# Eleven groups of unread matmuls added to TensorE's queue of a gated recurrence and convolution kernel

## Chip, cores and metric

The kernel runs on one core of one Trainium2 chip. The metric is the device time of one execution in microseconds (us), lower being better.

## What is computed

The input has 4 batches of 6336 steps by 256 channels. A gated linear recurrence runs along the steps, and its output goes through a gated unit with a causal convolution of five taps. Cut to what matters, the reference is:

```
log_a = 8 * sigmoid(r_gate) * log(a_base)            # a_base = sigmoid(a_param), per channel
a_t   = exp(log_a)
norm  = sqrt(max(1 - a_t*a_t, 1e-6))
h     = a_t[:, t] * h + (norm * sigmoid(i_gate) * x)[:, t]     # for each step t; y[:, t] = h
gate  = sigmoid(causal_conv(y, conv_w))              # five taps, per channel
out   = (gate * (y @ w_val)) @ w_out
```

## The kernel before

The 25344 rows (batch and step together) are cut into 51 windows `w` of 512 rows (256 for the first two and the last), and these into 28 chunks `c` of one or two windows. Inputs arrive with rows on the partitions. The recurrence needs channels on the partitions, so gates and products are turned by transposes on TensorE. The 256 channels are two halves `h`.

All work is issued in one order that is written out by hand: the string `ORDER` holds words such as `nt.3@6,7`, which is operation `nt` for chunk 3 in PSUM banks 6 and 7. Each word calls a function `op_...`. Every engine takes its own instructions in that order and waits at the first whose inputs are not ready; the DMA queue on SyncE (SP) does so too, with its loads and stores. The steps, with the engine and the line of the profile:

- `lr`, `li`, `lx` (SP, L290): load r_gate, i_gate and x of a window into rings of four windows. `st` (SP, L514) stores a window of the output.
- `ta`, `tb` (ScalarE, L308 and L311): tanh of half of r_gate and i_gate, for a chunk. `pp` and `up` (GpSimd, L318 and L330): 1 + tanh, and its product with x, into `uring`.
- `xp` and `uv` (TensorE L335, VectorE L344): the same product for the windows 1, 2 and 6, with x copied to PSUM by a float32 matmul with an identity.
- `tr` (TensorE, L355) transposes the tanh of r; `ex` (ScalarE, L371) makes a_t from it; `sq` (GpSimd, L379) squares it; `rt` (ScalarE, L398) makes the norm for a batch of chunks, with a table load before and after (L530).
- `nt` (TensorE, L413) transposes the norm back, `xg` (VectorE, L420) multiplies it into the products, `xt` (TensorE, L429) transposes those, and `sc` (VectorE, L451) runs the recurrence as a scan into `yring`.
- `cv` (TensorE, L463) is the convolution by matmuls with diagonal weights, `tg` (ScalarE, L470) its tanh, `vl` (TensorE, L478) is y @ w_val, `gv` (VectorE, L483) the gating, `ou` (TensorE, L493) the product with w_out; `cd` and `ca` (VectorE L501, ScalarE L503) copy the result from PSUM to be stored.

The eight PSUM banks are given to operations by the numbers behind the `@`. An operation that writes a bank waits until the earlier contents have been read.

Of the kernel before, what the change touches and what calls it, by code (L numbers as in the profile page):

```python
# [9 lines left out]
P = 128  # L10
# [30 lines left out]
s_wl.1 up.0 lx.1 ex.3.1 sq.3.0 lx.4 lx.3 tb.3 sq.3.1 ta.6 pp.4 sq.4.1 lr.13 ta.5 li.5 li.6 sq.4.0 li.7 xp.2@2,3  # L41
lr.14 pp.3 rt.0 tr.5.0@4,5 lx.6 uv.2 rt.2 up.4 nt.0@0 rt.1 xg.0 rt.3 xt.0@0,1 xp.1@2 sc.0.0 up.3 nt.1@3 lx.5 nt.2@0
uv.1 s_wl.0 xg.1 xg.2 xt.1@2,3 lx.7 sc.0.1 lr.12 nt.3@6,7 sc.1.0 lr.11 xt.2@0,1 sc.1.1 ex.5.0 xg.3 tr.5.1@2,3 li.8
sc.2.0 xt.3@6,7 ex.5.1 sq.5.0 cv.0@4,5 sc.2.1 tg.0 sc.3.1 cv.1@0,1 cv.2@4,5 tg.1 tb.4 s_wcast xp.6@0,1 sc.3.0 tg.2
li.10 li.9 pp.5 ta.8 vl.1@2,3 lx.10 vl.2@4,5 uv.6 sq.6.1 vl.0@6,7 ta.7 gv.2 lr.17 cv.3@0,1 lx.8 sq.6.0 gv.0
ou.2.0@4,5 gv.1 tb.5 ou.0.0@6 cd.2.0 ou.1.0@7 up.5 tr.7.0@2,3 tg.3 cd.0.0 st.2 vl.3@4,5 lr.16 cd.1.0 ex.7.0 sq.5.1
st.1 tr.7.1@0,1 gv.3 lr.15 st.0 nt.4@6,7 li.12 ex.7.1 pp.7 cv.4@2,3 xg.4 sq.7.0 ou.3.0@4,5 tg.4 vl.4@0,1 cd.3.0 tb.6
pp.8 xt.4@2,3 gv.4 st.3 sq.7.1 li.11 lr.18 sc.4.1 ou.4.0@0,1 li.13 lx.9 up.8 rt.4 sc.4.0 pp.9 up.7 cd.4.0 cv.6@2,3
st.4 vl.6@0,1 lx.12 pp.10 li.14 nt.5@4,5 lx.11 sq.8.0 cv.5@6,7 tg.6 xg.5 tb.7 up.10 gv.6 xt.5@4,5 ou.6.0@0,1 sc.5.0
ta.9 li.16 up.9 vl.5@2,3 tg.5 lr.19 cd.6.0 ta.10 pp.11 nt.6@6,7 gv.5 st.6 pp.12 li.15 xg.6 tb.8 ou.5.0@2,3 lr.22  # L50
up.11 tr.9.0@0,1 sc.5.1 ca.5.0 xt.6@6,7 ex.9.0 st.5 tr.9.1@2,3 lr.20 sc.6.0 lr.21 cv.7@4,5 ex.9.1 sq.8.1 up.12
cv.8@0,1 sc.6.1 tg.8 vl.7@2,3 pp.14 lx.16 lx.15 tg.7 nt.7@0,1 lx.14 sq.9.1 lx.13 tb.9 gv.7 cv.9@4,5 sq.10.1 xg.7
ou.7.0@2,3 tg.9 vl.9@6,7 cd.7.0 ta.11 sq.9.0 xt.7@4,5 gv.9 st.7 cv.10@2,3 li.20 ta.12 li.18 sc.7.0 pp.16 li.17
vl.8@6,7 sq.10.0 vl.10@0,1 tg.10 lr.26 li.19 gv.8 ou.9.0@2,3 pp.13 gv.10 ou.8.0@6,7 rt.5 up.14 cd.9.0 ou.10.0@0,1
tr.11.1@4 sc.7.1 st.9 up.16 lr.25 cd.10.0 cv.11@2,3 up.13 cd.8.0 st.10 nt.8@0,1 lr.23 tr.11.0@5 st.8 pp.15 xg.8
tg.11 vl.11@6,7 lr.24 lx.18 ex.11.1 up.15 xt.8@0,1 gv.11 lx.17 ex.11.0 nt.9@2,3 sc.8.0 sq.11.1 tb.10 cv.12@6,7
tr.12.0@5 xg.9 ex.12.0 li.22 pp.17 li.21 sc.8.1 tg.12 pp.18 ou.11.0@2,3 tb.11 xt.9@4,5 sq.11.0 vl.12@6,7 cd.11.0
cv.13@0,1 ta.14 sq.12.0 gv.12 st.11 li.23 cv.14@2,3 tg.13 sc.9.1 lr.29 pp.20 ou.12.0@6,7 ta.13 up.18 vl.13@0,1
cd.12.0 tr.12.1@5 tg.14 up.17 sc.9.0 st.12 tr.13.1@6,7 ex.12.1 lx.19 lx.20 nt.10@2,3 ex.13.1 li.24 sq.12.1 gv.13
tr.13.0@4,5 tb.12 xg.10 ou.13.0@0,1 sq.13.1 xt.10@2,3 cd.13.0 ex.13.0 cv.15@6,7 pp.22 sc.10.0 st.13 lx.21 cv.16@0,1  # L60
pp.19 lx.22 tg.15 lr.28 lr.30 sq.13.0 vl.15@4,5 tg.16 sc.10.1 li.25 vl.14@6,7 lr.27 pp.21 vl.16@0,1 gv.15 rt.6
sq.14.1 gv.14 ou.15.0@4,5 up.19 gv.16 cv.17@2,3 ou.14.0@6,7 cd.15.0 up.20 ou.16.0@0,1 cd.14.0 st.15 li.26 nt.11@4,5
cd.16.0 sq.14.0 lx.24 vl.17@6,7 tg.17 xg.11 st.14 lx.23 tb.13 st.16 gv.17 xt.11@4,5 up.21 cv.18@2,3 sc.11.1 sc.11.0
li.27 nt.12@6,7 li.28 ta.15 up.22 vl.18@0,1 tg.18 lr.32 pp.23 lr.31 ta.16 ou.17.0@2,3 pp.24 gv.18 up.24 tb.14 xg.12
tr.15.1@4,5 cv.20@0,1 cd.17.0 ex.15.1 xt.12@6,7 up.23 st.17 lr.33 tr.15.0@2,3 sc.12.0 lx.26 tg.20 lr.34 vl.20@4,5
sq.16.1 ex.15.0 cv.19@0,1 sc.12.1 sq.15.1 tg.19 ou.18.0@2,3 tb.15 cd.18.0 cv.21@6,7 pp.26 gv.20 st.18 sq.16.0
vl.19@2,3 tg.21 lx.25 lx.27 nt.13@0,1 ta.17 gv.19 lx.28 li.30 sq.15.0 vl.21@6,7 xg.13 li.29 ou.20.0@2,3 gv.21
xt.13@0,1 pp.27 rt.7 cv.22@4,5 cd.20.0 up.26 ou.21.0@6,7 sc.13.0 ou.19.0@2,3 pp.25 cd.19.0 up.25 sc.13.1 st.19 li.32
nt.14@2,3 up.27 lx.29 li.31 ta.18 lr.36 lx.30 cd.21.0 vl.22@0,1 lr.35 xg.14 pp.28 tg.22 tr.17.1@6,7 up.28 lr.38
tb.16 nt.15@2,3 gv.22 xt.14@4,5 lr.37 ex.17.1 tr.17.0@0,1 pp.29 xg.15 st.21 pp.30 sc.14.1 cv.23@2,3 ex.17.0 lx.31  # L70
up.29 cv.24@6,7 st.20 sc.14.0 tg.23 vl.23@0,1 sq.18.1 tb.17 li.34 ou.22.0@2,3 gv.23 up.30 li.33 nt.16@4,5 tg.24
cd.22.0 vl.24@0,1 lx.32 ta.19 ou.23.0@6,7 pp.31 xg.16 li.35 xt.15@2,3 sq.18.0 ca.23.0 gv.24 cv.26@4,5 li.36 ta.20
sc.15.0 sq.17.0 cv.25@0,1 st.22 tg.26 tr.19.0@6,7 sc.15.1 pp.32 lx.34 tg.25 vl.25@4,5 up.31 ex.19.0 tr.19.1@0,1
st.23 gv.25 ou.24.0@2,3 lr.41 ex.19.1 sq.19.0 xt.16@6,7 cd.24.0 ou.25.0@4,5 sc.16.0 st.24 cv.28@2,3 tb.18 lx.33
up.32 cv.27@0,1 tg.28 cd.25.0 tg.27 sq.19.1 vl.28@2,3 sc.16.1 st.25 lr.42 tb.19 vl.27@4,5 vl.26@0,1 sq.17.1 lr.39
gv.28 lr.40 gv.26 pp.34 ou.28.0@2,3 rt.8 lx.36 pp.36 gv.27 ou.26.0@0,1 pp.33 ou.27.0@4,5 up.34 cv.29@6,7 cd.28.0
cd.26.0 vl.30@2,3 up.33 cd.27.0 nt.17@0,1 tg.29 st.27 nt.18@4,5 pp.35 xg.17 lx.35 ta.22 st.28 vl.29@6,7 sq.20.1
xg.18 li.40 li.39 xt.17@0,1 li.38 gv.29 tr.22.0@4 sq.20.0 li.37 ta.21 sc.17.0 cv.30@6,7 st.26 up.36 tg.30 tr.21.1@5
sc.17.1 tr.21.0@0 lx.38 ex.22.0 xt.18@6,7 ex.21.0 tr.22.1@4 sq.22.0 lx.37 gv.30 ex.21.1 cv.31@0,1 lx.40 up.35
sc.18.0 ex.22.1 nt.19@2,3 lr.44 tg.31 cv.32@4,5 sq.22.1 sc.18.1 tb.21 ou.29.0@0,1 sq.21.1 tg.32 xg.19 ou.30.0@6,7  # L80
tb.20 vl.32@4,5 cd.29.0 sq.21.0 xt.19@2,3 gv.32 li.42 vl.31@0,1 lr.43 pp.38 li.41 cd.30.0 lx.39 lr.45 rt.9 up.38
gv.31 lr.46 sc.19.1 ou.31.0@0,1 st.29 pp.37 cv.33@6,7 pp.40 ou.32.0@4,5 cd.31.0 up.37 cd.32.0 cv.34@0,1 sc.19.0
nt.20@4,5 up.40 tg.33 lx.41 st.30 tg.34 li.43 vl.33@6,7 li.44 tb.22 xg.20 vl.34@0,1 pp.39 cv.36@2,3 nt.21@4,5 gv.33
up.39 ta.23 gv.34 ou.33.0@6,7 pp.41 ta.24 xg.21 lr.48 xt.20@0,1 lr.47 pp.42 st.31 cd.33.0 cv.35@4,5 lx.42 tg.36
sc.20.1 st.32 up.41 tr.23.0@6,7 tg.35 vl.35@2,3 ex.23.0 li.45 tr.23.1@4,5 gv.35 li.46 ex.23.1 sc.20.0 xt.21@6,7
sq.23.0 st.33 vl.36@2,3 tb.23 ou.34.0@4,5 sq.24.1 lx.43 gv.36 ou.35.0@0,1 sc.21.0 ca.34.0 cv.37@2,3 pp.44 ta.25
st.34 sq.23.1 cv.38@4,5 lx.44 sc.21.1 tg.37 tr.25.1@6 up.42 ex.25.1 nt.22@2,3 cd.35.0 tg.38 ou.36.0@6,7 sq.24.0
xg.22 sa.25.1 st.35 tr.25.0@0 lr.50 vl.38@4,5 lx.46 ex.25.0 cd.36.0 pp.43 xt.22@2,3 tb.24 gv.38 st.36 sq.25.0
cv.39@6,7 lx.45 sc.22.0 vl.39@4,5 tg.39 li.47 pp.46 vl.37@0,1 lr.49 up.43 ou.38.0@6,7 gv.37 rt.10 li.48 cd.38.0
ou.37.0@0,1 pp.45 sc.22.1 vl.40@6,7 up.44 gv.39 cv.40@2,3 up.46 cd.37.0 nt.23@4,5 st.37 cv.41@0,1 xg.23 tg.40 up.45  # L90
lx.48 st.38 lx.47 ta.27 tg.41 nt.24@2,3 gv.40 vl.41@4,5 xg.24 ta.26 tr.27.0@0 xt.23@6,7 gv.41 ex.27.0 ou.39.0@2,3
tb.25 sc.23.0 cv.42@4,5 ca.39.0 ou.41.0@0,1 pp.48 tg.42 sc.23.1 st.39 xt.24@2,3 pp.47 li.49 ca.41.0 li.50 tr.26.0@6
ou.40.0@4,5 up.48 ex.26.0 st.41 tr.26.1@0 sc.24.0 tr.27.1@1 ca.40.0 cv.44@6,7 ex.27.1 up.47 st.40 cv.43@4,5 ex.26.1
lx.49 sc.24.1 tg.44 sa.27.1 nt.25@0,1 sq.26.1 tg.43 vl.42@6,7 sq.27.0 tb.26 xg.25 vl.44@4,5 sq.26.0 tb.27 vl.43@2,3
gv.42 pp.50 xt.25@0,1 pp.49 gv.44 ou.42.0@6,7 rt.11 gv.43 ou.44.0@4,5 up.49 ca.42.0 sc.25.1 ou.43.0@2,3 ca.44.0
st.42 cv.45@6,7 ca.43.0 st.44 cv.46@4,5 sc.25.0 st.43 lx.50 nt.26@1 tg.46 vl.46@2,3 xg.26 tg.45 cv.47@4,5 gv.46
vl.47@6,7 tg.47 ou.46.0@2,3 gv.47 up.50 vl.45@4,5 ca.46.0 nt.27@6 ou.47.0@0,1 gv.45 st.46 xt.26@2,3 ca.47.0 xg.27
ou.45.0@4,5 sc.26.0 st.47 cv.48@0,1 ca.45.0 sc.26.1 xt.27@6,7 st.45 tg.48 vl.48@4,5 sc.27.1 cv.49@2,3 gv.48
vl.49@0,1 tg.49 sc.27.0 ou.48.0@4,5 gv.49 cv.50@2,3 ca.48.0 ou.49.0@0,1 tg.50 st.48 vl.50@4,5 ca.49.0 gv.50 st.49
ou.50.0@4 ca.50.0 st.50  # L100
"""


@with_exitstack
def kernel(
    ctx: ExitStack,
    tc: tile.TileContext,
    x: bass.AP,
# [8 lines left out]
    nc = tc.nc  # L117
# [36 lines left out]
    at = 4  # L154
    for c in range(NCH):
# [5 lines left out]
        if wrap:  # L161
            at = 4
# [7 lines left out]
        at = col  # L170
# [17 lines left out]
    with tc.manual_schedule():  # L188
# [11 lines left out]
        ident_b = const.tile([P, P], BF16, name="ident_b")  # L200
# [361 lines left out]
```

## Time and profile before

| quantity | value |
|---|---|
| median of 3 runs | 294.9 us (294.23 to 295.23) |
| profiled execution, its own time | 294.79 us |
| its span from the first to the last instruction | 292.8 us |
| mean granted TensorE clock | 0.983 |
| ScalarE busy | 274.1 us (94%) |
| VectorE busy | 246.9 us (84%) |
| GpSimd busy | 241.8 us (83%) |
| TensorE busy, matmuls | 241.5 us (83%), 2473 of them |
| DMA | 104.75 MB, 358 GB/s on average |

Busy times are of one profiled execution. The granted clock is TensorE's share of full speed; it is a mean over the span and was near one half in two short stretches. TensorE's matmuls are pipelined, so consecutive ones overlap and the time of one is longer than the step between two. Names in the profile are PE for TensorE, PEld for its weight loads, DVE for VectorE, ACT for ScalarE, POOL for GpSimd and SPq for the DMA queue of SyncE.

### The profile page before, as it was taken

To read this page: it belongs to the slowest core of one execution; us is meant where nothing else is said; L and a number is where in the kernel's file an instruction comes from. 1 tells how busy PE (TensorE), PEld (TensorE's weight loads), DVE (VectorE), ACT (ScalarE), POOL (GpSimd) and SP (SyncE) were. 2 spreads that over 40 slices of the span, in tenths; PEclk is the share of its full clock that TensorE was granted. 3 is DMA by queue.
4 is the path that set the end of the run, shared out by engine and by line. 5 is a ranking of instruction groups with operands and counts; after the bars stand their busy time and mean duration, and the time that the engine had idled before them with its cause. 6 is when DMAs were issued, how large, how long until landed. Compare 5 with 4: busy or idle time off the path is not lost.

```text
span 292.8 us, 6228 instructions
## 1 busy us (share of the span) xinstructions
PE 241.5 (83%) x2473; PEld 166.1 (57%) x2497; DVE 246.9 (84%) x214; ACT 274.1 (94%) x197; POOL 241.8 (83%) x161
## 2 busy tenths in 40 slices
PE   2234889859798888889897999898699997999993
PEld 1231656627665657465575676566466664776562
DVE  5001799766999999999999999979999999999891
ACT  5999979999799999999999999999999999999754
POOL 1659469998999989999999999999999799497100
PEclk9999999968999999999997999999999999999999
DMA  7999988999899999999999999999999999785554
GB/s 249 381 396 408 397 321 334 390 384 366 290 409 388 379 419 373 365 397 407 419 378 360 368 412 414 418 382 408 354 334 418 416 409 406 242 311 200 212 216 179
DMA packets 29995, 104.75 MB, mean 358 GB/s; under 512 B 3335, under 2 KB 3854, under 8 KB 29966
## 3 DMA queue, kind: packets, MB, share of 16 engines
q1 hardware_dynamic: 29952, 104.35, 92.9%
q8 instruction: 19, 0.31, 0.4%
q14 instruction: 10, 0.08, 0.1%
q10 hardware_dynamic: 14, 0.01, 0.0%
HBM read 78.39 MB, written 25.95 MB: 356 GB/s over the span
## 4 chain that ended last, share of the span: by engine, by line
POOL 33%; PE 30%; DVE 16%; issue 10%; DMA 7%; ACT 3%; SPq 1%; DVEq 0%; POOLq 0%; ACTq 0%
POOL uring L330 14%; POOL ering L379 12%; PE banks L463 9%; DVE yring L451 7%; POOL tbring L318 7%; PE banks L493 5%; PE banks L478 5%; PE banks L413 4%; DVE tgring L483 4%; DMA rring<-in_r_gate_dram 4%; DMA xring<-in_x_dram 3%; DVE oring L501 2%; PE banks L355 2%; PE banks L335 2%; PE banks L429 2%
## 5 line engine op out<-in xcount | busy, mean ns | idle before, releaser
L330 POOL TENSOR_TENSOR uring<-tbring,xring 128x1024 bf16<-128x1024 bf16 (+1 forms) x48 | 100.9, 2117 | 11.0 <-DMA xring<-in_x_dram 10.5
L451 DVE TENSOR_TENSOR_SCAN yring<-aring,yring,banks 128x1024 bf16<-128x1024 f32 (+5 forms) x54 | 106.0, 1990 | 0.2
L379 POOL TENSOR_TENSOR ering<-aring 128x1024 f32<-128x1024 f32 (+2 forms) x54 | 91.8, 1716 | 15.5 <-ACT aring L371 15.4
L463 PE MATMUL banks<-yring,diag 64*64 64x512 bf16 (+7 forms) x1080 | 63.9, 366 | 7.0 <-DVE yring L451 6.4
L483 DVE SCALAR_TENSOR_TENSOR tgring<-tgring,banks 128x1024 bf16<-128x1024 bf16 (+1 forms) x51 | 59.4, 1183 | 4.6 <-PE banks L478 2.4
L493 PE MATMUL banks<-wo,tgring 128*128 128x256 bf16 x396 | 51.3, 274 | 10.7 <-DVE tgring L483 8.0
L371 ACT ACTIVATE aring<-banks,khf 128x2048 f32<-128x2048 bf16 (+3 forms) x38 | 54.1, 1471 | 1.5 <-PE banks L355 1.4
L318 POOL TENSOR_SCALAR tbring<-tbring 128x1024 bf16<-128x1024 bf16 (+1 forms) x48 | 49.1, 1033 | 7.4 <-ACT tbring L311 7.4
L470 ACT ACTIVATE tgring<-banks 128x1024 bf16<-128x1024 f32 (+1 forms) x51 | 50.6, 1007 | 3.7 <-PE banks L463 3.6
L493 PEld LDWEIGHTS <-tgring 128*128 128x128 bf16 x396 | 41.3, 114 | 22.1 <-DVE tgring L483 14.2
L478 PE MATMUL banks<-yring,wv 128*128 128x512 bf16 (+4 forms) x192 | 49.6, 368 | 2.4 <-ACT tgring L470 0.3
L308 ACT ACTIVATE taring<-rring 128x2048 bf16<-128x2048 f32 (+2 forms) x28 | 47.5, 1717 | 2.7 <-DMA rring<-in_r_gate_dram 2.7
L311 ACT ACTIVATE tbring<-iring 128x2048 bf16<-128x2048 f32 (+2 forms) x28 | 48.0, 1722 | 0.0
L463 PEld LDWEIGHTS <-diag 64*64 64x64 bf16 x1080 | 29.0, 107 | 31.1 <-issue 14.6
L398 ACT ACTIVATE ering<-ering 128x4096 bf16<-128x4096 f32 (+5 forms) x15 | 44.7, 3018 | 0.1
L501 DVE COPY oring<-banks 128x1024 f32<-128x1024 f32 (+1 forms) x36 | 42.1, 1186 | 1.6 <-PE banks L493 1.1
L355 PE MATMUL banks<-ident_b,taring 128*128 128x128 bf16 x396 | 31.2, 234 | 9.3 <-ACT taring L308 7.5
L420 DVE TENSOR_TENSOR uring<-banks,uring 128x2048 bf16<-128x2048 bf16 (+2 forms) x28 | 30.5, 1094 | 9.3 <-PE banks L413 8.5
L355 PEld LDWEIGHTS <-taring 128*128 128x128 bf16 x396 | 27.1, 106 | 15.9 <-ACT taring L308 9.5
L413 PE MATMUL banks<-ident,ering 128*128 128x128 f32 x198 | 30.5, 298 | 2.7 <-ACT ering L398 2.2
L478 PEld LDWEIGHTS <-wv 128*128 128x128 bf16 x216 | 20.2, 99 | 21.5 <-issue 7.5
L413 PEld LDWEIGHTS banks<-ident,ering 128*128 128x128 f32 x198 | 26.6, 208 | 9.7 <-ACT ering L398 3.9
(43 smaller groups left out, 122.3 us busy)
## 6 DMA issues: line engine op xcount, KB each, us to landing
rring<-in_r_gate_dram SPq DMA_DIRECT2D x48, 512.0 KB, 7.7
iring<-in_i_gate_dram SPq DMA_DIRECT2D x48, 512.0 KB, 7.5
xring<-in_x_dram SPq DMA_DIRECT2D x48, 512.0 KB, 7.3
out_dram<-oring SPq DMA_DIRECT2D x48, 512.0 KB, 5.5
rring<-in_r_gate_dram SPq DMA_DIRECT2D x3, 256.0 KB, 4.2
iring<-in_i_gate_dram SPq DMA_DIRECT2D x3, 256.0 KB, 5.2
xring<-in_x_dram SPq DMA_DIRECT2D x3, 256.0 KB, 8.5
out_dram<-oring SPq DMA_DIRECT2D x3, 256.0 KB, 6.3
```

The lines of the kernel that those rows point to most:

```text
L318: nc.gpsimd.tensor_scalar(out=t, in0=t, scalar1=1.0, scalar2=1.0, op0=ALU.mult, op1=ALU.add)
L330: nc.gpsimd.tensor_tensor(out=u, in0=t1, in1=xt, op=ALU.mult)
L355: nc.tensor.transpose(out=bank[:, o:o + P], in_=taring[:, place(w, NTR), j, h * P:(h + 1) * P], identity=ident_b[:])
L371: nc.scalar.activation(out=dst, in_=src, func=ACT.Exp, scale=khf[:, h:h + 1], bias=khf[:, h:h + 1])
L379: nc.gpsimd.tensor_tensor(out=e, in0=a, in1=a, op=ALU.mult)
L413: nc.tensor.transpose(out=bank[:, k:k + P], in_=ering[:, e + q:e + wins[w] // 2:nq], identity=ident[:])
L451: nc.vector.tensor_tensor_scan(out=yring[:, h, col:col + o1 - o0], data0=aring[:, h, a_at[c] + o0:a_at[c] + o1], data1=xT[:, o0:o1], initi ...
L463: nc.tensor.matmul(out=gp[oh * 64:oh * 64 + 64, h, a:b], lhsT=diag[half * 64:half * 64 + 64, h, k, :], rhs=yring[half * 64:half * 64 + 64, ...
L470: nc.scalar.activation(out=tgring[:, w % NTG, :, 0:wins[w]], in_=live.pop(("gp", w))[:, :, 0:wins[w]], func=ACT.Tanh, scale=0.5)
L478: nc.tensor.matmul(out=val[:, m, a:b], lhsT=wv[:, hk, m * P:(m + 1) * P], rhs=yring[:, hk, col:col + b - a], start=(hk == 0), stop=(hk == ...
L483: nc.vector.scalar_tensor_tensor(out=tgring[:, w % NTG, :, 0:wins[w]], in0=tgring[:, w % NTG, :, 0:wins[w]], scalar=1.0, in1=live.pop(("va ...
L493: nc.tensor.matmul(out=ops[:, j * D:(j + 1) * D], lhsT=gv[:, hk, j:wins[w]:J], rhs=wo[:, hk, :], start=(hk == 0), stop=(hk == H - 1))
```

## The change

A new operation `wm` issues five bf16 matmuls of the identity with itself, each 128 by 512, into one PSUM bank. Nothing reads the results, and the number behind `wm` is not used. Eleven words are added to `ORDER`. The order of the other words is the same. From nt.3 on, all but tr.5.1 and cv.0 have their banks renumbered one for one: 0 and 1 become 6 and 7, 2 and 3 become 4 and 5, 4 and 5 become 2 and 3, and 6 and 7 become 0 and 1.

```
+        def op_wm(k, at):
+            for _ in range(5):
+                nc.tensor.matmul(out=banks[:, at], lhsT=ident_b[:], rhs=ident_b[:].unsqueeze(1).to_broadcast([P, 4, P]),
+                                 start=True, stop=True)
```

On TensorE's queue, the groups stand between these neighbours (banks as they are after the change):

```
tr.3.0@4,5 tr.3.1@2,3 | wm.10@6 wm.5@6 wm.3@6 wm.9@6 wm.6@6 | xp.2@2,3 tr.5.0@4,5 nt.0@0
vl.4@6,7 xt.4@4,5 ou.4.0@6,7 | wm.4@0 wm.12@0 | cv.6@4,5 vl.6@6,7 nt.5@2,3 cv.5@0,1 xt.5@2,3
xt.5@2,3 ou.6.0@6,7 vl.5@4,5 | wm.8@2 | nt.6@0,1 ou.5.0@4,5 tr.9.0@6,7
vl.8@0,1 vl.10@6,7 ou.9.0@4,5 | wm.2@2 | ou.8.0@0,1 ou.10.0@6,7 tr.11.1@2
cv.22@2,3 ou.21.0@0,1 ou.19.0@4,5 | wm.16@6 | nt.14@4,5 vl.22@6,7 tr.17.1@0,1
vl.32@2,3 xt.19@4,5 vl.31@6,7 | wm.18@2 | ou.31.0@6,7 cv.33@0,1 ou.32.0@2,3
```

## The prediction

> **What bounds the kernel now.** I read the busy times first, then the slices, then the chain of waits, then the timeline around each place where the change puts matmuls.
>
> ```profile
> PE 241.5 (83%) x2473; PEld 166.1 (57%) x2497; DVE 246.9 (84%) x214; ACT 274.1 (94%) x197; POOL 241.8 (83%) x161
> PEclk9999999968999999999997999999999999999999
> DMA  7999988999899999999999999999999999785554
> ```
>
> ScalarE (ACT) is busy 274 of 292.8 us. In windows of 5 us it is idle at the start (0 to 45 us), for 0.46 us in 70 to 75 and 1.32 us in 75 to 80, for 0.36 in 100 to 105, and then hardly at all until 265. GpSimd (POOL) is as full from 105 to 225, and the chain of waits runs over it there. From 235 to 289 the chain lies on a gapless TensorE (PE). So an idle stretch of ACT or POOL before 105 us is time that nothing later wins back or loses: whatever goes there comes off the end. The question is whether the change removes such stretches. The timeline shows three on ACT that TensorE ends (by line: L335 is xp, L371 ex, L413 nt, L420 xg, L463 cv, L470 tg, L503 ca):
>
> ```profile
> 25.94 3.75 PE L335 MATMUL banks<-xring,ident 128*128 128x512 f32 x4 [7.94 <-DMA xring<-in_x_dram]
> 42.09 1.98 PE L335 MATMUL banks<-xring,ident 128*128 128x512 f32 x4
> 37.85 2.06 ACT L371 ACTIVATE aring<-banks,khf 128x2048 f32<-128x2048 bf16 x1 [1.06 <-PE banks L355]
> 41.12 0.60 ACT L470 ACTIVATE tgring<-banks 128x512 bf16<-128x512 f32 x1 [0.71 <-PE banks L463]
> 62.43 2.35 PE L463 MATMUL banks<-yring,diag 64*64 64x512 bf16 x20 [3.43 <-DVE yring L451]
> 68.24 1.23 DVE L420 TENSOR_TENSOR uring<-banks,uring 128x2048 bf16<-128x2048 bf16 x1 [4.75 <-PE banks L413]
> 76.32 1.01 ACT L503 COPY oring<-banks 128x1024 f32<-128x1024 f32 x1 [1.78 <-PE banks L493]
> ```
>
> Columns are start, duration, instruction and, in brackets, the idle time before it and what ended it. The same four passes of xp last 3.75 us at 25.94 and 1.98 at 42.09: after 7.94 us of idling TensorE runs at half speed. No clock is recorded before the first change of state, so the 1.00 printed there says nothing; the durations do.
>
> The clock moves on a grid. The profile shows it at 0.50 from 61.00 to 67.8 and from 156.6 to 160.0, and these edges fit one grid of 3.41 us. The windows view of TensorE alone, cut on that grid (stretch, length, busy us, granted clock, DMA):
>
> ```profile
> 26.87:30.28 3.41, 3.41 (x12) 1.00 1.02 406
> 57.59:61.00 3.41, 1.06 (x8) 1.00 1.02 369
> 61.00:64.41 3.41, 1.98 (x20) 0.50 0.98 398
> 64.41:67.83 3.42, 3.42 (x15) 0.50 1.03 374
> 71.24:74.65 3.41, 2.23 (x16) 1.00 0.74 282
> 153.16:156.57 3.41, 1.45 (x13) 1.00 0.93 377
> 156.57:159.99 3.42, 3.20 (x18) 0.50 0.99 341
> ```
>
> Windows with 1.06 and 1.45 us of work were followed by half clock, one with 2.23 was not; 3.20 to 3.42 us brought full clock, 1.98 did not. The durations around 30 us fit a rise at 30.28.
>
> **The change part by part.** It removes nothing and keeps every other instruction in order; the PSUM banks are renamed from nt.3 on. It adds 11 groups of five 128x512 bf16 matmuls, 55 in all, with no DMA and no reader. A step between such matmuls comes from the vl rows: at full clock four take 1.03 us with 0.379 for one, so (1.03-0.379)/3 = 0.217 us; at half clock 1.89 and 0.634, so 0.419. A group is 1.1 us warm, 2.1 cold; all 55 are 12 to 23 us of TensorE work.
>
> *First five groups (25 matmuls).* They stand behind tr.3.1, which ends at 18.00, and ahead of xp.2, which waits for its load until 25.94. Bank 6 is untouched before, so they start at 18.0. The window 16.63 to 20.04 holds 1.37 us of transposes and then these, so it is full and the clock rises at 20.04: 4.9 matmuls cold, 20.1 x 0.217 = 4.4 us, end at 24.4. Transposes do count in this: of the 3.20 us in 156.57 to 159.99, about 1.9 are transposes, and the clock rose, while 1.98 us of plain matmuls alone had not been enough. The Trainium skill (TensorE: Matmul & The Clock Gate, Part 4) says full clock does not engage for transpose mode; that row disagrees, and by the page the end would be 26.05, which is no loss worth a term.
>
> Then xp.2 starts at 25.94 as before and takes 1.98 instead of 3.75 (-1.77), and tr.5.0 behind it 0.89 instead of 1.24 (-0.35): nt.0 is 2.1 us earlier, at 28.65. Its other input, rt.0, is the first of four square roots in 27.82 to 33.43 and done by 28.5. VectorE follows by 2.1: xg.0 at 29.15 for 31.27. Then rt.3, which ends at 33.43 and does not move, limits nt.3; from 33.5 that gives xg.3 at 34.65 for 36.74, still 2.1. (The renaming adds a wait here: nt.3 now takes banks 0 and 1, which xg.2 and sc.0.1 must have read. By the moved times sc.0.1 ends at 33.3, so it costs nothing; with VectorE at its old times nt.3 would start at 35.5 instead of 34.7, and xt.2, tr.5.1 and ex.5.1 behind it would be 0.8 later.) On ACT, ex.5.0 stays at 34.74 (table load after rt.3), but ex.5.1, tg.0 and tg.1 no longer wait: 34.74+2.06+2.06+0.59+0.60 = 40.05 for tb.4 instead of 41.61. **Term one: -1.56 us.** GpSimd waits for tb.4 (2.13 us of idling), so it gets the same, and so does the SP queue, where li.10 and li.9 stand behind tb.4.
>
> *wm.4 and wm.12.* They stand ahead of cv.6, in the idle 3.43 us from 59.00 (bank 0 was read out by 54.4). Ten warm matmuls are 2.2 us: hidden, with 1.2 to spare. Any window of 3.41 us now holds over 2.1 us of work, so the clock stays up: cv.6, vl.6 and nt.5 take 1.22+0.97+1.21 instead of 2.35+1.82+1.55. Against 62.43 that is 65.83 instead of 68.15, -2.3 for xg.5 (its square root ends at 64.09, early enough at 64.62). VectorE is gapless from there to gv.5, ou.5.0 follows it, and the 1.78 us that ACT waits for ou.5.0 are covered. **Term two: -1.78 us.** What is late next on ACT is nothing until tr.12.0 at 103.8 (0.36).
>
> *wm.8* stands ahead of nt.6, where TensorE is not idle, and its bank 2 is read by sc.5.0 until 72.9: nt.6 then ends at 75.1, and xg.6 starts at 75.08 behind gv.5. Zero to +0.1; with that cover gone +1.1. *wm.2* moves ou.8.0 and ou.10.0 by about 1 us; their copies run at 96, two us later: zero. *wm.16* lies in the 1.96 us before 155.91, where it fills a window of 1.45 us to 2.5 and saves the half clock up to 160; nobody waited for it (xg.14 and ex.17.1 start behind their own engines): zero. *wm.18* lies in 2.37 us of idling before 212.37: zero. **Sum: -3.34 us.**
>
> What can cut it is DMA. Its share is 1.0 from 80 to 245, with idle stretches of 2.1 us in 40 to 45 and 1.2 in 70 to 80. Both come from SP waiting (for tb.4, and for the copy ahead of st.6) and move with the engines: 1.56 + about 1.2 = 2.8. So the gain lies between 2.8 and 3.34; I take 3.1. The profiled execution took 294.79 us (span 292.8 and 2.0 around it), 0.1 under the median of 294.9, so both bases give **291.7**.
>
> **A rule weighed.** A gap of 1.5 us is left between 24.4 and 25.94, and the window 23.45 to 26.87 then has 1.9 us of work, between the 1.45 that cooled and the 2.23 that did not. The row at 153.16 cooled with a gap of 1.97 us. The Trainium skill (the same page, "Why this matters for your kernels") calls gaps up to about 3 us safe; that row goes against it. By the page the gap is harmless and the sum stands; by the rows it may cool.
>
> **Rivals.**
> 1. *The clock falls again at 26.87.* Half of xp.2 is warm then: -0.9 instead of -1.56, total 2.4 after the cut: 292.4. For: the unsettled 1.9 us. Against: it is nearer to 2.23.
> 2. *One stage gives nothing back*: for instance the 1.78 us come back as a wait of ACT for loads, as DMA is full. Then only one term is left, 293.0 to 293.3.
> 3. *DMA is the real bound* and both terms turn into waits for loads: 294.8. For: share 1.0. Against: after 75 us no engine waits for a load in the waits view.
> 4. *Slower: identity by identity does not lift the clock.* The monitor may not count a product that is nearly all zeros. Then 25 x 0.419 = 10.5 us, to 28.5, and xp.2 starts 2.5 us late and cold; at 59.0 ten take 4.2 us instead of fitting in 3.43, +0.8. Total +3.3: 298.1. It decides if the clock is still at half at 25.9. Against: the transposes, which also stream an identity, counted.
> 5. *The matmuls do not run there*: an extra wait on bank 6 would push all of them behind 25.94. No earlier instruction uses that bank, so I give it no weight.
>
> **How the numbers follow.** Both terms, 291.7: 0.50. Rival 1: 0.12. Rival 2: 0.12. Rival 3: 0.09. Rival 4, with smaller mishaps of its sign: 0.17. About 0.3% (0.9 us) is what a measurement of this kernel can tell from no change: faster 0.74, same 0.09, slower 0.17. The range takes in the likeliest case with an uncut sum and a little over (290.4) and rivals 1 to 3 (295.0); it leaves out the slower case. The likeliest case's own range is 291.0 to 292.3.
>
> **What would show it.** In the changed profile: 55 more matmuls; the four passes at about 25.9 lasting 2 us; tb.4 starting near 40.0; no clock of 0.5 between 55 and 70; the wait of ACT before ca.5.0 gone; ACT at 76 us some 3.3 us ahead; and the chain still on POOL and then PE. Wrong would be: xp.2 starting after 26.7, POOL or ACT with new waits for loads after 80 us, or VectorE waiting for nt.6.

## The result and the profile after

The changed kernel takes 290.17 us (median of 4 runs, 290.0 to 290.72) against 294.56 us for the kernel before (4 runs, 293.69 to 295.23). The ratio is 0.9856, with a 95% interval of 0.9824 to 0.9887: some 4.4 us faster. The forecast was 291.7 us with a range of 290.4 to 295.0. The direction was right; the gain was larger than the forecast 3.2 us, and the time lies 0.23 us below the range.

The profiled execution of the changed kernel took 290.72 us, with a span of 288.6. Its page, first the busy times, then the slices:

```profile
PE 250.6 (87%) x2552; PEld 169.4 (59%) x2552; DVE 247.0 (86%) x214; ACT 273.7 (95%) x197; POOL 241.5 (84%) x161
PEclk9999999999999999999999999999999999999998
DMA  7999999999999999999999999999999999885554
```

TensorE has 9 us more work, the other engines have the same within half a microsecond, and no slice but the last has a reduced clock. The weight loads (PEld) are 55 more, as many as there are added matmuls; the matmul records are 79 more, so some matmuls are missing from the earlier trace. The timeline (start, duration, instruction, idle time before it and what ended that) at the two places of the forecast; the line numbers behind the new operation are five higher in this kernel, and those of the experiments' kernels lie two lower before it and three higher behind it:

```profile
17.44 6.77 PE L362 MATMUL banks<-ident_b 128*128 128x512 bf16 x25
25.47 1.96 PE L335 MATMUL banks<-xring,ident 128*128 128x512 f32 x4 [1.27 <-DMA xring<-in_x_dram]
34.27 4.01 ACT L376 ACTIVATE aring<-banks,khf 128x2048 f32<-128x2048 bf16 x2
38.17 1.18 ACT L475 ACTIVATE tgring<-banks 128x512 bf16<-128x512 f32 x2
44.08 1.92 ACT L308 ACTIVATE taring<-rring 128x2048 bf16<-128x2048 f32 x1 [0.22 <-DMA rring<-in_r_gate_dram]
56.58 2.32 PE L362 MATMUL banks<-ident_b 128*128 128x512 bf16 x10
60.17 1.27 PE L468 MATMUL banks<-yring,diag 64*64 64x512 bf16 x20 [1.27 <-DVE yring L456]
63.47 1.22 DVE L425 TENSOR_TENSOR uring<-banks,uring 128x2048 bf16<-128x2048 bf16 x1 [2.24 <-PE banks L418]
72.40 1.00 ACT L508 COPY oring<-banks 128x1024 f32<-128x1024 f32 x1
```

The first 25 matmuls are over by 24.2 us, 1.27 us before xp's load comes, and the four passes of xp take 1.96 us. The two exponentials at 34.27 and the two tanh at 38.17 now follow without a gap (before: 1.06 and 0.71 us). The ten matmuls at 56.58 leave 1.27 of the 3.43 idle us; cv.6 takes 1.27 us. The copy on ScalarE at 72.40 has no wait ahead of it (before: 1.78). A new wait of 0.22 us for a load stands at 44.08.

The windows of TensorE on the clock's grid in this execution, where the first recorded change to full clock is at 19.88 us (stretch, length, busy us, granted clock, DMA share, GB/s; before the first change the clock is not recorded):

```profile
13.05:16.47 3.42, 2.60 (x23) 1.00 1.03 411
16.47:19.88 3.41, 3.41 (x18) 1.00 1.03 383
23.29:26.71 3.42, 2.15 (x8) 1.00 1.04 405
57.43:60.84 3.41, 2.14 (x20) 1.00 1.01 390
207.61:211.02 3.41, 2.78 (x34) 1.00 0.95 372
```

The first of these did not raise the clock, the second did. After that no window before 282 us holds less than 1.98 us (at 30.12), and the clock stays up until 286.

**Where the time came from.** ScalarE issues the same 197 instructions in the same order in every kernel here, so the same instruction can be looked up in two profiles and its starts subtracted. I take five: ex.5.0 (34.74 us before), tb.5 (47.92), the second tanh after ca.5.0 (82.21), a tanh of r (232.93) and the last copy (289.20). The differences between neighbouring points are the lead that a stage gains (negative is earlier). Each row, here and below, is one profiled execution:

| kernel profiled | up to ex.5.0 (loads) | start, to 48 | middle, to 82 | late, to 233 | rest | last copy |
|---|---|---|---|---|---|---|
| changed | -0.47 | -1.55 | -2.10 | -0.02 | -0.02 | -4.16 |

Between 82 and 233 us the lead moves by 0.02. The -0.47 us lies in waits for the first loads: 0.35 of it is there at 13.3 us, before the first added matmul, and the rest at the next wait for a load, at 24.59.

### The profile page after: what moved, and what is told of

The parts are those of the page before. It is cut to its first block, busy times and chain, and to the rows that moved or that the text cites. A ratio compares the mean times of both kernels' runs of the same rounds, so it can differ in the third digit from the quotient of the medians.

```text
span 288.6 us, 6363 instructions
## 1 busy us (share of the span) xinstructions
PE 250.6 (87%) x2552; PEld 169.4 (59%) x2552; DVE 247.0 (86%) x214; ACT 273.7 (95%) x197; POOL 241.5 (84%) x161
## 4 chain that ended last, share of the span: by engine, by line
POOL 31%; PE 20%; DMA 15%; DVE 12%; ACT 12%; issue 7%; SPq 2%; DVEq 0%; ACTq 0%; POOLq 0%
POOL uring L330 14%; POOL ering L384 11%; DMA xring<-in_x_dram 8%; POOL tbring L318 6%; PE banks L468 6%; DMA iring<-in_i_gate_dram 6%; DVE yring L456 5%; DVE tgring L488 4%; PE banks L483 4%; PE banks L498 3%; PE banks L418 3%; ACT aring L376 3%; ACT tbring L311 3%; ACT ering L403 2%; SPq L290 2%
## 5 line engine op out<-in xcount | busy, mean ns | idle before, releaser
L468 PE MATMUL banks<-yring,diag 64*64 64x512 bf16 (+7 forms) x1080 | 62.9, 361 | 4.6 <-DVE yring L456 3.6
L355 PE MATMUL banks<-ident_b,taring 128*128 128x128 bf16 x396 | 30.2, 230 | 9.4 <-ACT taring L308 7.2
L425 DVE TENSOR_TENSOR uring<-banks,uring 128x2048 bf16<-128x2048 bf16 (+2 forms) x28 | 30.4, 1093 | 6.7 <-PE banks L418 5.7
L355 PEld LDWEIGHTS <-taring 128*128 128x128 bf16 x396 | 26.1, 103 | 15.1 <-ACT taring L308 9.2
L418 PE MATMUL banks<-ident,ering 128*128 128x128 f32 x198 | 29.7, 292 | 1.9 <-DVE yring L456 0.9
L418 PEld LDWEIGHTS banks<-ident,ering 128*128 128x128 f32 x198 | 25.9, 207 | 9.1 <-ACT ering L403 3.5
```

The lines of the kernel that those rows point to most:

```text
L355: nc.tensor.transpose(out=bank[:, o:o + P], in_=taring[:, place(w, NTR), j, h * P:(h + 1) * P], identity=ident_b[:])
L418: nc.tensor.transpose(out=bank[:, k:k + P], in_=ering[:, e + q:e + wins[w] // 2:nq], identity=ident[:])
L468: nc.tensor.matmul(out=gp[oh * 64:oh * 64 + 64, h, a:b], lhsT=diag[half * 64:half * 64 + 64, h, k, :], rhs=yring[half * 64:half * 64 + 64, ...
```

## Experiments

In all of them only words of the hand-written order are left out, except in one that replaces the matmuls. The banks stay renamed as in the change. The table at the end of this section gives the stages of each.

**1. The first five groups alone.**

```
-wm.4@0 -wm.12@0 -wm.8@2 -wm.2@2 -wm.16@6 -wm.18@2
```

> Only the first five groups are kept; the other six are left out, the banks stay renamed. Theory A (the two removed ScalarE waits carry the gain, each by itself): about 1.9 us of 4.4 remain, ratio to before 0.993 to 0.995, 292.3 to 293.0 us; the clock falls to half near 60 us again, and ScalarE waits 1.5 to 2 us before ca.5.0 as before. Theory B (the extra over the forecast comes from the renamed banks or from the four small groups): less than 1 us is gained. Theory C (the stages depend on each other, so that an earlier start shifts the later idle stretch and the clock stays up by itself): over 3.5 us is gained.

Measured: 292.92 us against 294.16 (ratio 0.996, 0.9939 to 0.998). The time is in Theory A's range, the ratio just above it, and the clock fell at 60.1 us. But the profile has more in it than that theory. The wait before the copy is only 0.89 us; the clock was down for one grid window instead of two,

```profile
72.66 1.01 ACT L506 COPY oring<-banks 128x1024 f32<-128x1024 f32 x1 [0.89 <-PE banks L496]
```

and the lead of 3.67 us that ScalarE had at 82 us had shrunk to 1.58 by 233 us.

**2. Only the two groups ahead of cv.6.**

```
-wm.10@6 -wm.5@6 -wm.3@6 -wm.9@6 -wm.6@6 -wm.8@2 -wm.2@2 -wm.16@6 -wm.18@2
```

> Only wm.4 and wm.12, ahead of cv.6, are kept. Theory A: the start is as before (four passes of xp in 3.75 us), no half clock between 55 and 70, the wait before ca.5.0 gone: -1.9 to -2.1 us, ratio 0.993, 292.4 to 292.9 us. Theory B: less than 1 us. Theory C: less than 1 us, because the gain needs the earlier start.

Measured: 293.03 us against 294.16, ratio 0.9976 (0.9945 to 1.0007): above Theory A's range of 292.4 to 292.9, and not told from no change by the time alone. The profiled execution, at 295.47 us, was the slowest of its twelve. It shows the wait before ca.5.0 gone (0.00), and the start 0.37 us worse than in the profile of before. The clock fell once, at 212.2 us, and 2.3 us of lead were lost between 82 and 233, 1.6 of them from 217 to 226 us, behind that fall.

**3. The two together, seven groups.**

```
-wm.8@2 -wm.2@2 -wm.16@6 -wm.18@2
```

> The first five groups with wm.4 and wm.12; the four later groups are left out. Theory A: all of the gain, ratio to before 0.985 to 0.987, within 0.3 us of the changed kernel (290.0 to 290.7). Theory B with the four groups as the cause: 1 us slower than the changed kernel or more.

Measured: 291.51 us against 294.16 (0.9913, 0.9882 to 0.9943). This was the miss that mattered. The changed kernel stands at 0.9856, and at 0.9883 in experiment 10: the seven groups look about 1 us slower, as Theory B had it for the later groups, not equal, though the intervals overlap. The profile shows a place where one of the four later groups may be missed. In the timeline of the seven groups:

```profile
207.73 1.90 PE L496 MATMUL banks<-wo,tgring 128*128 128x256 bf16 x8 [2.37 <-DVE tgring L486]
209.56 1.99 PE L466 MATMUL banks<-yring,diag 64*64 64x512 bf16 x20
212.58 1.22 DVE L504 COPY oring<-banks 128x1024 f32<-128x1024 f32 x1 [1.53 <-PE banks L496]
213.80 1.02 ACT L473 ACTIVATE tgring<-banks 128x1024 bf16<-128x1024 f32 x1 [0.57 <-PE banks L466]
```

and in its windows:

```profile
204.23:207.64 3.41, 1.13 (x6) 1.00 0.97 357
207.64:211.05 3.41, 3.32 (x24) 0.50 0.87 327
```

In the changed kernel the same place reads:

```profile
205.97 1.24 PE L362 MATMUL banks<-ident_b 128*128 128x512 bf16 x5
208.24 1.06 PE L498 MATMUL banks<-wo,tgring 128*128 128x256 bf16 x8 [1.03 <-DVE tgring L488]
209.23 1.27 PE L468 MATMUL banks<-yring,diag 64*64 64x512 bf16 x20
210.35 2.41 DVE L506 COPY oring<-banks 128x1024 f32<-128x1024 f32 x2
```

Without wm.18, TensorE idles 2.37 us ahead of ou.31.0; the window that ends at 207.64 holds 1.13 us of work, and the clock falls there. The product and the convolution take 1.90 and 1.99 us instead of 1.06 and 1.27, VectorE's second copy waits 1.53 us where in the changed kernel two copies follow each other, and ScalarE, which waits for two later convolutions, ends 1.54 us of lead poorer.

**4. The four later groups alone.**

```
-wm.10@6 -wm.5@6 -wm.3@6 -wm.9@6 -wm.6@6 -wm.4@0 -wm.12@0
```

> Only the four later groups wm.8, wm.2, wm.16 and wm.18 are kept. Theory A: no change, ratio 0.999 to 1.001 (wm.8 may cost 0.1 us). The half clock near 157 us is gone, that near 61 us stays. Theory B: faster by 0.5 us or more.

Measured: 293.63 us against 294.16 (0.9992, 0.9968 to 1.0015): no change that can be told. The profile is nearly that of before: the clock down from 61.1 to 67.9 us, up at 157 us, and not down at 212 either, where the profile of before had no fall to take away.

**5. The renamed banks alone.**

```
-wm.10@6 -wm.5@6 -wm.3@6 -wm.9@6 -wm.6@6 -wm.4@0 -wm.12@0 -wm.8@2 -wm.2@2 -wm.16@6 -wm.18@2
```

> No added matmul at all; only the banks are renamed from nt.3 on. Theory A: no change, ratio 0.999 to 1.001: nt.3 now waits for sc.0.1 and is up to 0.8 us later with VectorE at its old times, which could cost up to 0.8 us through ex.5.1 (ratio 1.0 to 1.003). Theory B (the renaming is a cause of the gain): faster by 0.5 us or more.

Measured: 293.97 us against 293.74 (0.9996, 0.997 to 1.0022). The renaming does nothing to the time that can be seen. But this profile is of the same work as the one of before and looks different: the clock rose at 31.1 instead of 30.3, ex.5.1 waited 1.56 us instead of 1.06, the clock was down for one window at 61.8 instead of two, and down again at 212.0, where the profile of before shows no fall. The renaming is not what lengthens that wait: with renamed banks and a rise at 30.4 us (experiment 4) it was 1.02.

**6. Three groups in place of five.**

```
-wm.9@6 -wm.6@6 -wm.4@0 -wm.12@0 -wm.8@2 -wm.2@2 -wm.16@6 -wm.18@2
```

> Three of the first five groups and nothing else. They end near 22.0, 3.5 us ahead of xp, so a stretch of the clock's grid of 3.41 us has little work and the clock falls again while xp runs or before. If the clock falls on little work in a grid window: between nothing and half of the gain of the five groups, 0 to -1 us, and the passes of xp are partly or all at half speed. If a gap must be well over 3 us: all of the gain of the five groups, -1.6 to -1.9 us, with four passes in 2.0 us.

Measured: 293.03 us against 293.74 (0.9975, 0.9947 to 1.0003), not told from no change. The start gained 0.41 us instead of 1.55 to 1.9. The windows:

```profile
19.58:22.99 3.41, 2.69 (x13) 1.00 0.95 324
22.99:26.41 3.42, 0.08 (x1) 1.00 1.03 411
26.41:29.82 3.41, 3.41 (x5) 0.50 1.03 412
```

The three groups raised the clock at 19.58, but a gap of 4.06 us followed, a whole window was empty, and it fell 0.08 us after xp had begun. The groups have to reach up to the work that they are for.

**7. Transposes instead of matmuls.**

```
-                nc.tensor.matmul(out=banks[:, at], lhsT=ident_b[:], rhs=..., start=True, stop=True)   # 5 a group
+                nc.tensor.transpose(out=bank[:, o:o + P], in_=ident_b[:], identity=ident_b[:])      # 16 a group
```

> In place of the first five groups, 80 transposes of the identity, 128x128 bf16, on the same bank; the six later groups are left out. If transposes raise the clock: at half clock until about 20 us, then fast, end near 24, xp in 2.0 us, about the gain of the five groups of matmuls (-1.6 to -1.9 us). If they do not raise it (as the Trainium skill, TensorE: Matmul & The Clock Gate, Part 4, says): 80 x 0.114 = 9.1 us, end at 26.6, xp 1.0 us late and at half speed: slower by 0.5 to 1 us than before.

Measured: 293.99 us against 293.74 (1.0014, 0.9988 to 1.0039). The gain of the five groups did not come; a loss of 0.5 to 1 us can't be told from no change. From the timeline:

```profile
17.52 5.29 PE L362 MATMUL banks<-ident_b 128*128 128x128 bf16 x80
26.19 3.41 PE L333 MATMUL banks<-xring,ident 128*128 128x512 f32 x4 [3.39 <-DMA xring<-in_x_dram]
```

The 80 transposes took 5.29 us, not 9.1, and the clock rose at 18.88, behind a window that held transposes alone: they raise it. But they ended at 22.8, 3.4 us ahead of xp, and it fell again at 25.70, as in experiment 6. My count of 80 was too small to test the time: it was worked out from their duration at half clock.

**8. One group ahead of cv.6 instead of two.**

```
-wm.12@0 -wm.8@2 -wm.2@2 -wm.16@6 -wm.18@2
```

> The first five groups and one of the two groups ahead of cv.6 (wm.4), nothing else. It fills 1.1 of about 3.5 idle us, so a grid window around 57 to 61 holds about 2.1 us of work instead of 1.06. If 2.1 is enough (a window of 2.23 was in the trace of before): no half clock there and the whole gain, ratio 0.985 to 0.987. If it is not: as with the first five groups alone, 0.993.

Measured: 292.37 us against 293.74 (0.9952, 0.9932 to 0.9972). The condition was put wrongly, since it took the place of the grid from another execution. TensorE idled 2.35 us after the group, and the grid lay such that the window 56.61 to 60.02 held 1.06 us of work; the clock fell at 60.02, the wait before ca.5.0 was 0.91, and it fell again at 210.2.

**9 to 12. The late group told apart.** After experiment 3 the theory was new, and four kernels on one chip tested it. First, the eight groups without wm.8, wm.2 and wm.16:

```
-wm.8@2 -wm.2@2 -wm.16@6
```

> The first five groups, wm.4, wm.12 and wm.18; wm.8, wm.2 and wm.16 are left out. Theory D, formed after the earlier runs: there is a third place, near 210 us, where the clock falls in some executions (with the seven groups it fell at 207.6, a copy on VectorE waited 1.5 us longer for its matmuls, and 1.5 of 4.6 us of lead were lost by 226 us); the forecast held wm.18 to be worth nothing since the profile of before happened to show no fall there. Then these eight groups are within 0.3 us of the changed kernel run beside them, and show no fall at 207 to 212. If wm.8, wm.2 or wm.16 matter instead: about 1 us slower than the changed kernel, like the seven groups.

The changed kernel itself beside it:

> The changed kernel as it is, all eleven groups, beside the others on this chip. 290.0 to 290.7 us as in its first runs, with a spread well below that of the kernel before, if the spread of before comes from where the clock's grid lies.

Measured: 290.03 us (289.85 to 290.99) for the eight groups and 290.35 (289.81 to 291.27) for all eleven, against 293.94 (292.31 to 296.26) before; ratios 0.9874 (0.9839 to 0.9909) and 0.9883 (0.9847 to 0.9919). Eight groups give all of the gain, as far as these intervals tell. In their profile the clock fell at 151.7 for one window, since wm.16 is missing,

```profile
148.32:151.73 3.41, 1.45 (x13) 1.00 0.89 363
151.73:155.14 3.41, 3.41 (x19) 0.50 1.03 369
```

and no lead was lost there: the table shows 0.07 us from 82 to 233.

wm.18 alone:

```
-wm.10@6 -wm.5@6 -wm.3@6 -wm.9@6 -wm.6@6 -wm.4@0 -wm.12@0 -wm.8@2 -wm.2@2 -wm.16@6
```

> Only wm.18. Theory D: no fall near 212; faster than before by the mean loss there, 0 to 1.5 us by where the grid lies in each execution, 0.3 to 1.0 us in the median (ratio 0.9965 to 0.999). By the forecast (worth nothing): ratio 0.9995 to 1.0005. As the profiled execution of before had no fall there, this profile may show no difference by itself.

Measured: 294.13 us against 293.94, ratio 1.0013 (0.9985 to 1.0042). Not the gain of 0.3 to 1.0 us that I expected, though the interval does not exclude 0.4. There was no fall at 212 in its profile. So the fall near 210 costs 1.5 us in an execution like the profiled one of the seven groups. On the average wm.18 may be worth something like the 0.3 to 0.4% between 0.9913 and 0.9874 to 0.9883, but these are runs on two chips and their intervals overlap; in the kernel before it is not shown to be worth anything.

All later groups without the first five:

```
-wm.10@6 -wm.5@6 -wm.3@6 -wm.9@6 -wm.6@6
```

> All later groups, without the first five. This removes term one alone: 1.6 to 1.9 us slower than the changed kernel, 291.8 to 292.6 us; xp in 3.4 to 3.75 us, tb.4 some 1.6 us later, no half clock after 31 us. If the later gain needs the earlier start: more than 2.5 us slower than the changed kernel.

Measured: 292.51 us against 293.94 (0.9943, 0.9916 to 0.997): in the range of times, and 2.16 us slower than the changed kernel beside it, between the 1.6 to 1.9 of the one theory and the 2.5 of the other. In its profile the clock rose only at 31.7 us and ex.5.1 waited 1.84 us, so its start was 0.78 us worse than in the profile of before; its middle gained the whole 2.09.

The stages of all profiles, as leads against the profile of before (the few hundredths missing to the last column lie behind 233 us, 0.2 to 0.3 us in three rows):

| groups in the kernel | loads | start | middle | late | last copy | falls of the clock near 60 and near 210 |
|---|---|---|---|---|---|---|
| none, banks renamed (5) | -0.54 | 0.50 | -1.18 | 1.62 | 0.39 | one window; yes |
| first five (1) | -0.88 | -1.90 | -0.89 | 2.08 | -1.42 | one window; yes |
| first five and one (8) | -0.64 | -1.90 | -0.89 | 1.58 | -1.58 | one window; yes |
| the two of the middle (2) | -0.55 | 0.37 | -1.52 | 2.30 | 0.57 | no; yes |
| seven (3) | -0.64 | -1.90 | -2.10 | 1.54 | -3.11 | no; yes |
| three first (6) | 0.35 | -0.41 | -0.17 | -0.04 | -0.30 | two windows; no |
| transposes first (7) | -0.82 | 0.37 | -0.32 | -0.05 | -0.83 | two windows; no |
| four later (4) | 0.24 | -0.04 | -0.03 | -0.03 | 0.13 | two windows; no |
| wm.18 alone (11) | -0.65 | -0.72 | -0.32 | 0.17 | -1.54 | two windows; no |
| six later (12) | -0.06 | 0.78 | -2.09 | 0.12 | -1.27 | no; no |
| eight (9) | -0.97 | -1.90 | -2.09 | 0.07 | -4.92 | no; no |
| eleven, again (10) | -0.17 | -1.59 | -2.11 | 0.00 | -3.60 | no; no |

## Why the forecast was right and where it was wrong

**The two terms.** The mechanisms were as forecast and are additive: the seven groups have the start of the first five (-1.90) and the middle of the six later ones (-2.1) in one profile. Term one was put at -1.56 and measured -1.55 in the changed kernel, but that agreement is luck: two errors of a third of a microsecond cancel. There 0.33 us of a larger lead went with the 0.22 us wait for a load at 44.08, and without that wait it is -1.90 (eight groups). And the sum of durations in that step was too long by 0.33 us, since consecutive instructions of ScalarE overlap: 4.01 and 1.18 us for the two pairs, against 2.06+2.06 and 0.59+0.60, and 4.98 from the first start to tb.4 against 5.31. Term two was put at -1.78 and measured -2.10; the wait itself is 1.78, and the rest lies in the instructions around it: the copy's start moves 1.88 us and the tanh behind it another 0.18.

**The cut for DMA fell elsewhere.** I took 0.24 us off for a full DMA. From 82 to 233 us the lead did not shrink; what loads took from ScalarE here is the 0.33 us at 44.08, inside term one. The length of the queue changed too: the median time from issue to landing went from 7.7, 7.5 and 7.3 us for r, i and x to

```profile
rring<-in_r_gate_dram SPq DMA_DIRECT2D x48, 512.0 KB, 7.9
iring<-in_i_gate_dram SPq DMA_DIRECT2D x48, 512.0 KB, 8.2
xring<-in_x_dram SPq DMA_DIRECT2D x48, 512.0 KB, 7.9
```

and from 36 us on ScalarE waited for one load only, those 0.22 us. GpSimd did wait longer for one: 1.99 us at 40.29 for w_val (0.35 before), so that it led by only 1.03 us from 43 to 70 us, and not by as much as ScalarE, as I had put it. It made that up where it used to wait, 1.09 us for a load at 73.49 and 0.7 to 1.0 us for ScalarE at 81.33 and 103.52, and then led by 4.11. Loads are now 15% of the chain that ended last, against 7% before; 18.5 us of that are from 154.7 to 173.2 us, where the chain of before has none. What a still larger lead would be worth is not shown.

**The steps that failed.** The forecast took a gain of 3.1 us; the medians give 4.4. The sum was short at two places, and the base it was taken from moved.

First, both terms were too small by a third of a microsecond: -1.56 where the start gives -1.90, and -1.78 where the middle gives -2.10. With the 0.33 us for the load, the pair of profiles gives 3.7 us without the first loads.

Second, "wm.18 lies in 2.37 us of idling before 212.37: zero" used one execution's clock as if it were the kernel's. The falls and rises come on a grid of 3.41 us that lies differently in each execution. In the profile of before, the idle time was split between two windows of 2.23 us of work each, and nothing fell. Its row in the timeline, and its windows:

```profile
212.37 1.06 PE L493 MATMUL banks<-wo,tgring 128*128 128x256 bf16 x8 [2.37 <-DVE tgring L483]
207.77:211.18 3.41, 2.23 (x14) 1.00 0.81 291
211.18:214.60 3.42, 2.23 (x29) 1.00 0.92 329
```

The same 2.37 us stand in all eight profiles without wm.18. Five of them show a fall near 210, and each loses 1.5 to 1.6 us of lead between 217 and 226 us; the other three, that of before among them, do not. None of the six profiles with wm.18 (the changed kernel twice) falls. But not all of these six needed it. The windows that hold wm.18's 1.24 us, in the changed kernel's first profile and in that of experiment 10, are

```profile
204.20:207.61 3.41, 2.91 (x16) 1.00 0.86 306
205.32:208.74 3.42, 2.29 (x11) 1.00 0.81 310
```

Without the group the second would have held about 1.05 us, the first about 1.67, which is above all windows that brought a fall. So the group kept the clock up in the second execution and was probably not needed in the first.

The base: 294.9 was the median of three runs, and with a fourth it is 294.56. That 0.34 us is more than the 0.23 us by which the time lies below the range. (294.9 less 3.1 is also 291.8; the 291.7 goes by the profiled execution.)

One profile misleads elsewhere too. The profile of before had a start that was 0.4 to 0.8 us better than in experiments 2, 5 and 12 and 0.7 worse than in 11, all without a group ahead of xp, and a middle with two windows at half clock, like four of the other profiles without the two middle groups, where three have one. The kernel with renamed banks alone does the same work, and against its profile the changed kernel's lead without the loads is 4.6 us, not 3.7. How much of the 0.7 us between the medians and the pair of profiles is the late place, how much the other places of the grid and how much the landing of the first loads, which moves the lead by -0.97 to +0.35 us between these profiles, stays open: the late group by itself gave no measurable gain.

**The other groups.** wm.8, wm.2 and wm.16 at zero: right, as the eight groups show. wm.8 waited 0.39 us for VectorE, and xg.6 on VectorE waited 0.11 us for nt.6 behind it, the sign that the forecast named as wrong; ScalarE's lead shows nothing of it, -2.10 us in the middle with wm.8 and -2.09 without.

**The rivals.** The clock falling again at 26.87 did not happen: the window held 2.15 us of work, and the gap was 1.27 us. Experiments 6 and 7 show what it would have cost: 0.41 us gained in the one, 0.37 lost in the other. The rival on the slow side, that products of an identity are not counted, fell with the first profile and with experiment 7. Rivals 2 and 3, in which loads take a term or both back, fell too: of the lead at 82 us ScalarE keeps all to the last copy. (The reading that no engine waits for a load after 75 us holds up to 265 us; GpSimd waits for x at 268 and 276 us, before the change as after it.) An extra wait on bank 6 did not occur: the matmuls began right behind tr.3.1.

**The rule weighed.** The forecast let the row speak against the Trainium skill (TensorE: Matmul & The Clock Gate, Part 4), which has transposes not engage full clock. The runs settle it for the transposes that this kernel issues, which the profile records as matmuls: in the profile with wm.18 alone a window with such transposes only raised the clock,

```profile
14.49:17.90 3.41, 2.74 (x24) 1.00 1.02 400
17.90:21.31 3.41, 0.00 (x0) 1.00 1.01 384
21.31:24.73 3.42, 0.00 (x0) 0.50 1.02 403
```

since the first recorded change to full clock is at 17.90, and the empty window after it brought it down at 21.31. The same page's advice that gaps up to about 3 us do no harm ("Why this matters for your kernels") is not borne out either: gaps of 1.96 us (before 155.91, in the profile of before) and 2.37 us brought a fall, by the window into which they came.

## What to carry to other kernels

A wait that the profile puts down to TensorE can be the clock, and the cure is work of no use in TensorE's idle time, placed so that it reaches up to the matmuls that others wait for. Judge a gap by the least work that any stretch of 3.41 us over it can hold, not by the window in which one profile happened to put it, and look at every place where that least is below some 1.6 us, whether or not the one profile shows a fall. Such a fall costs time only where an engine on the path waits for the slow matmuls: the one at 151.7 us in the eight groups cost nothing. Where an engine without idle time sets the end, a wait removed ahead of it comes off the end whole; look for it in the start of the same instruction in both profiles.

## What the runs showed of the clock

Taking the windows of all fourteen profiles on their own grids: every fall came behind a window with 1.51 us of TensorE work or less, and no window with 1.61 or more brought one (one with 1.45 did not either). Rises came behind windows with 2.74 us and more, and the fullest window at half clock that brought none held 2.76. The half-clock windows between 2.0 and 2.78 us all lie before the first recorded change, where half clock is read from the durations. So, as an estimate from these figures, it takes about 80% of a window to raise the clock and under about 45% to lose it. The kernel before spread over 4 us in its 23 runs beside the last four kernels (292.31 to 296.26) and the changed kernel over 1.5 in six (289.81 to 291.27). That fits a grid that no longer matters once the clock is held up, but it is not shown: the landing of the first loads differs between executions too, and fewer runs spread less.
